# Eight gate/value pairs by seven products, weight bits joined in PSUM, and a down product that starts with two output blocks side by side

## The chip, the cores and the metric

One core of a Trainium2 chip runs the whole program. The metric is the device time of one execution in microseconds (us); the median of three runs counts. The engines are PE (TensorE: matmuls, whose results land in PSUM), DVE (VectorE), ACT (ScalarE), POOL (GpSimd) and SP, which issues the loads and stores. Each engine works through its own queue in order; an instruction that has to wait for another engine holds everything behind it in its queue.

## The reference

Attention with a bias from a small network (2 batches, 8 heads, 576 positions, head size 64), then two feed-forward blocks on the 1152 resulting rows of width 512:

```
x = attention(q, k, v, w1, b1, w2)                     # 1152 x 512
xn = x / rms(x) * rms_g
g, val = xn @ w_gate, xn @ w_val                       # 512 -> 1536, twice
y = (silu(g) * val) @ w_out                            # 1536 -> 512
r = max(y @ w_in, 0)                                   # 512 -> 2048
out = (s * r * r + b) @ w_out2                         # 2048 -> 512
```

The weights come as 64-bit floating-point numbers and are turned into 32-bit ones on the chip.

## The kernel before

The first 178 us are attention. After that PE works through the feed-forward blocks with weights as the stationary operand and 384 rows of the activations (a third of the 1152, called j = 0, 1, 2) as the moving one. To keep precision every operand is split in two, a rounded part (`hi`) and the remainder (`lo`), and each 128-deep step takes three matmuls: hi·hi, hi·lo and lo·hi (`mm3`, lines 588 to 593).

**The gated stage** makes 12 pairs m = 0 to 11 of one gate block and one value block (128 outputs each). Its smallest step is `prod` (line 613): six matmuls of 128x384, half the depth of 512. A pair done in the plain way takes 2 blocks x 3 thirds x 2 halves = 12 such steps (`whole`, line 693). `seven` (line 706) takes a fast matrix multiplication for the thirds j = 0 and 1: seven products in place of eight, of sums of weights (`t_sums`, `t_split`, lines 653 and 668) and of sums of activations (made once, `s_view`, in the buffer `reg`); with the four plain steps of j = 2 that is 11 steps: p1, p2, p5, p6, gate half, p7, gate half, value half, value half, p4, p3. Products p1, p6, p7 and p4 add up in one PSUM bank `a`, and between them ACT copies out what stands there (`snap`, line 646): p6 waits for the copy of p1, p7 for the copy of p6, p4 for the copy of p7. The copy of p6 has one step of PE in which to be made. `MIXED` (line 675) lists the pairs done so: 3, 5, 7, 9, 11.

Each block's weights are a *unit* of 512 KB, 2m the gate's and 2m + 1 the value's; units 24 on are those of the later products. A unit passes a load by SP (`w_fetch`), ACT's absolute value and POOL's clamp (`w_clamp`, lines 379 and 380), three DVE steps that join the bits (`bits_of`, lines 387, 388, 390, all in place in the tile `wa`), ACT's rounding to `whi` (line 402) and POOL's subtraction to `wlo` (line 405). `prep(q, p)` (line 677) sets which of these stands at step p of the pair ahead of pair q, with one table for a pair in `MIXED`, one for a pair behind one of these, one for the rest. `later(d, fn)` puts a piece of work into the queues d steps on; `up_gated` calls `due()` (the pieces whose time has come), then `prep`, then the PE step.

The product of gate and value is made on DVE (`times`, line 633). For m < `KEPT` = 7 it is split at once: DVE multiplies into the PSUM bank, ACT rounds from there, DVE subtracts. For the other five pairs DVE writes a plain tile, and `narrow` (line 796) splits it later, at steps 1 to 5 of the down product, 1152 columns at a time.

**The down product** (`down`, line 834) takes for each output block m = 0 to 3 the twelve results in three chunks i of four; a step (`slot`) is 12 matmuls of 384 columns. Before the change all chunks of a block are done before the next block. The second feed-forward block runs in two halves, each of eight `up_sq` blocks and a `down` of two chunks.

`bank()` (line 549) hands out the eight PSUM banks in turn: three of `psB`, four of `psC`, and `po`, the one bank of `psO` that attention used for its output.

Of the kernel before, what the change touches and what calls it, by code (L numbers as in the profile page):

```python
# [8 lines left out]
F32 = mybir.dt.float32  # L9
F32R = mybir.dt.float32r  # L10
I32 = mybir.dt.int32
U64 = mybir.dt.uint64
AF = mybir.ActivationFunctionType
ALU = mybir.AluOpType
# [3 lines left out]
P = 128  # L18
# [6 lines left out]
NT = B * S  # L25
DM = H * D
NKC = DM // P
# [24 lines left out]
def tile_kernel(ctx: ExitStack, tc: tile.TileContext, q, k, v, ltab, lg, cst, cst2, rms_g, wg, wv, wo, win, wo2, s_p, b_p, out):  # L52
    nc = tc.nc
# [24 lines left out]
    psO = pool(ctx, "psO", 1, space=PSUM)  # L78
# [41 lines left out]
    def batches(u):  # L120
        tt = TILES[u // 4]
        return [tt % 2] if tt < 8 else [0, 1]
# [106 lines left out]
    pos = {}  # L229
# [54 lines left out]
    def values_mm(u):  # L284
        hp = u % 4
        bs = batches(u)
        if hp == 0:
            pos[u // 4] = psO.tile([P, 512], F32, name="po")
        po = pos[u // 4]
        cols = P // len(bs)  # L290
        tl = pts.pop((u, 2))
        pm = [pts.pop((u, e)) for e in range(2)]
        for bi, b in enumerate(bs):
            c0 = bi * cols
            vt = vs[b * NP + hp]
            for c in range(NQC):
                for o in range(0, P, 32):
                    e, d = divmod(o, D)
                    dst = po[o:o + 32, hp * P + c0:hp * P + c0 + cols]
                    w, a = (vt[:, 4 * e + c, d:d + 32], pm[e][:, c * P + c0:c * P + c0 + cols]) if c < 4 else \  # L300
                        (vt[:, 8 + e, d:d + 32], tl[:, c0:c0 + cols])
                    nc.tensor.matmul(dst, w, a, start=c == 0, stop=c == NQC - 1, tile_position=(0, o))  # L302
# [51 lines left out]
    units = []  # L354
    for m in range(12):
        units += [wg[m], wv[m]]
    for m in range(NKC):
        units += [wo[m, 0, i] for i in range(3)]
    for half in range(2):
        units += [win[half * 8 + m] for m in range(8)]  # L360
        for m in range(NKC):
            units += [wo2[m, half, i] for i in range(2)]
    wst = {}
    wab = {}
    wpools = {}
# [17 lines left out]
    def bits_of(n):  # L383
        raw, w = wst[n]
        wst[n] = w
        a = w
        yield nc.vector.tensor_scalar(a, a, 3, 0x3FFFFFF8, op0=ALU.logical_shift_left, op1=ALU.bitwise_and)  # L387
        yield nc.vector.scalar_tensor_tensor(out=w, in0=raw[:, :, 1], scalar=-0x40000000, in1=a,  # L388
                                             op0=ALU.bitwise_and, op1=ALU.bitwise_or)
        yield nc.vector.scalar_tensor_tensor(out=w, in0=raw[:, :, 0], scalar=29, in1=w,  # L390
                                             op0=ALU.logical_shift_right, op1=ALU.bitwise_or)

    def w_bits(n):
# [3 lines left out]
    def w_split(n):  # L397
        if n < len(units):
            w = wst[n]
            hi = wpools["sp"].tile([P, 4 * P], F32R, name="whi")  # L400
            lo = wpools["sp"].tile([P, 4 * P], F32R, name="wlo")
            nc.scalar.copy(hi, w.bitcast(F32))  # L402
            step = 2 * P if n in FIRST_DOWN else 4 * P
            for c in range(0, 4 * P, step):
                nc.gpsimd.tensor_tensor(out=lo[:, c:c + step], in0=w[:, c:c + step].bitcast(F32),  # L405
                                        in1=hi[:, c:c + step].bitcast(F32), op=ALU.subtract)
            wst[n] = hi, lo
# [58 lines left out]
    for s in range(-2, NU + 1):  # L466
# [54 lines left out]
        if s == 26:  # L521
# [5 lines left out]
            reg = reg_p.tile([P, 6 * NT], F32R, name="reg", tag="reg")  # L527
# [13 lines left out]
    ff_p = pool(ctx, "ff", 1)  # L541
    t_p = ring(ctx, "t", 3)
    turn = [0]
    cur = [0]

    def ff(i, dtype=F32R):
        return ff_p.tile([P, NT], dtype, name="f", tag=f"f{i}")

    def bank():
        turn[0] += 1  # L550
        if turn[0] % 8 == 7:
            return psO.tile([P, 512], F32, name="po")
        if turn[0] % 2:
            return psB.tile([P, 512], F32, name="b")
        return psC.tile([P, 512], F32, name="c")

# [12 lines left out]
    def later(d, fn):  # L569
        late.append([d, fn])  # L570
# [9 lines left out]
    def slot(i):  # L580
        ahead(i)
        due()

    def take():
        w = wst.pop(cur[0])
        return w

    def mm3(ps, w, c, ah, al, first, last):
        hi, lo = w
        ws = slice(c * P, (c + 1) * P)  # L590
        nc.tensor.matmul(ps, hi[:, ws], ah, start=first, stop=False)  # L591
        nc.tensor.matmul(ps, hi[:, ws], al, start=False, stop=False)  # L592
        nc.tensor.matmul(ps, lo[:, ws], ah, start=False, stop=last)  # L593
# [7 lines left out]
            mm3(ps, w, c, src[0][:, c, cols(j)], src[1][:, c, cols(j)], c == 0, c == NKC - 1)  # L601
        return ps

    KEPT = 7
    ffs = {}
    sgs = {}

    def act_pair(m):
        if m not in ffs:
            ffs[m] = [ff(2 * m), ff(2 * m + 1)] if m < KEPT else [ff(2 * KEPT + m - KEPT, F32)]  # L610
        return ffs[m]
# [60 lines left out]
        nc.gpsimd.tensor_tensor(out=lo, in0=t, in1=hi.bitcast(F32), op=ALU.subtract)  # L672
        tsp[q, i] = hi, lo

    MIXED = (3, 5, 7, 9, 11)

    def prep(q, p):
        n = 2 * q
        if q in MIXED:
            do = {1: [(w_bits, n)], 2: [(w_clamp, n + 1)], 3: [(w_fetch, n + 2), (w_split, n)], 4: [(w_bits, n + 1)],  # L680
                  5: [(w_fetch, n + 3)], 6: [(t_sums, q, 0)], 7: [(t_sums, q, 1)], 8: [(t_split, q, 0)],
                  10: [(t_split, q, 1)], 11: [(w_split, n + 1)]}
        elif q - 1 in MIXED:
            do = {0: [(w_clamp, n)], 1: [(w_clamp, n + 1)], 2: [(w_bits, n)], 3: [(w_fetch, n + 2)],
                  4: [(w_bits, n + 1)], 5: [(w_fetch, n + 3)], 6: [(w_split, n)], 8: [(w_split, n + 1)],
                  9: [(w_clamp, n + 2)]}
        else:
            do = {1: [(w_bits, n)], 2: [(w_clamp, n + 1)], 3: [(w_fetch, n + 2), (w_split, n)], 5: [(w_bits, n + 1)],
                  6: [(w_fetch, n + 3)], 8: [(w_split, n + 1)], 9: [(w_clamp, n + 2)]}
        for fn, *arg in do.get(p, ()):  # L690
            fn(*arg)

    def whole(m, f, j):
        st = []
# [76 lines left out]
    def up_gated(n_m):  # L771
        last = NTT - 1
        subs = [(m, fn) for m in range(n_m)
                for fn in (seven(m) if m in MIXED else [h for f in range(2) for j in range(NJ) for h in whole(m, f, j)])]
        order = [0, 1, 2, 3, 6, 7, 8, 9, 12, 13, 4, 5, 10, 11]
        subs[:len(order)] = [subs[i] for i in order]
        start = [2 * 2 * NJ * m - len([x for x in MIXED if x < m]) for m in range(n_m + 1)]
        for t, (m, fn) in enumerate(subs):
            at = max(x for x in range(n_m) if start[x] <= t)
            due()  # L780
            prep(at + 1, t - start[at])
            if t in LATER:
                LATER[t][0](LATER[t][1])
            fn()
            if t == 0:
                finish_t(last)
                finish_b(last)
                finish_s(last)
                finish_n(last)
            if t == 6:  # L790
                finish_c(last)
        cur[0] = 2 * n_m
        place = {7: (reg, 0), 8: (reg, 1), 9: (reg, 2), 10: (14, 15), 11: (16, 17)}
        acts = [ffs[m] for m in range(KEPT)]

        def narrow(m, src):
            a, b = place[m]
            if m < 10:
                hh, hl = (reg[:, (2 * b + i) * NT:(2 * b + i + 1) * NT] for i in range(2))
            else:  # L800
                hh, hl = ff(a), ff(b)
            nc.scalar.copy(hh, src)
            nc.vector.tensor_tensor(out=hl, in0=src, in1=hh.bitcast(F32), op=ALU.subtract)
            acts[m] = hh, hl

        acts += [None] * (n_m - KEPT)
        for i, m in enumerate(range(KEPT, n_m)):
            later(i + 1, lambda m=m: narrow(m, ffs[m][0]))
        return acts

    sq_at = iter(list(range(16)) + [16, 17, 18] + list(range(13)))
# [21 lines left out]

    def down(acts, emit, tail=False):
        n = len(acts)
        for m in range(NKC):
            parts = [cols(j) for j in range(NJ)]
            if tail and m == NKC - 1:
                parts[1:] = [slice(TJ, NT - TAIL_N), slice(NT - TAIL_N, NT)]
            pss = [bank()[:, :cs.stop - cs.start] for cs in parts]  # L840
            for i in range(n // 4):
                w = take()
                for j, cs in enumerate(parts):
                    slot(j)
                    for c in range(4):
                        a = acts[4 * i + c]
                        mm3(pss[j], w, c, a[0][:, cs], a[1][:, cs],
                            i == 0 and c == 0, i == n // 4 - 1 and c == 3)
                    if i == n // 4 - 1:
                        emit(m, cs, pss[j])  # L850
                cur[0] += 1

    sg_p = ring(ctx, "sg", 4)
    ts_p = pool(ctx, "ts", 1)
# [1 line left out]
    acts = up_gated(12)  # L856
# [112 lines left out]
```

## Time and profile before

| what | value |
|---|---|
| three runs | 606.63, 607.23, 609.87 us; median 607.23 |
| the profiled execution | 606.63 us, of which the span of the trace is 604.9 us |
| PE busy in the span | 596.2 us (99%) |
| PEld, DVE, ACT, POOL busy | 534.3, 426.1, 324.5, 224.9 us |

PE's busy share counts matmuls that overlap one another, so it says little by itself. More telling is the distance from one matmul's start to the next one's, and the places where PE stood idle. All rows in the section on rows come from the one profiled execution.

### The profile page before, as it was taken

How to read it: one execution, taken by the hardware profiler on the slowest of the kernel's cores; microseconds unless marked ns; L12 is line 12 of the kernel's file. 1: busy time of each engine (PE TensorE's matmuls, PEld its weight loads, DVE VectorE, ACT ScalarE, POOL GpSimd, SP SyncE). 2: the span in 40 equal slices, each digit the busy share in tenths (PEclk: the TensorE clock that was granted, in tenths of full speed). 3: DMA queues.
4: the chain of work that ended last, by engine and by line, in shares of the span. 5: the costliest groups of instructions: out<-in, count | busy, mean ns of one | idle time of the engine just before them, and what ended most of it. 6: DMA issues, size and time to landing. Idle time of an engine off the chain costs nothing.

```text
span 604.9 us, 13376 instructions
## 1 busy us (share of the span) xinstructions
PE 596.2 (99%) x5400; PEld 534.3 (88%) x5400; DVE 426.1 (70%) x765; ACT 324.5 (54%) x670; POOL 224.9 (37%) x201
## 2 busy tenths in 40 slices
PE   8999999999999999999999999999999999999997
PEld 5466666667779999999999999999999999999997
DVE  7977888976877887676467745648887535888851
ACT  7887887887765355544346322245555235555210
POOL 0424334623437754344444233322224333222420
PEclk9999999999999999999999999999999999999999
DMA  7998544564112233223223133222223422222431
GB/s 215 267 320 234 158 149 142 159 209 136 37 40 69 70 104 105 71 74 130 76 70 105 71 105 104 70 71 70 69 71 106 139 70 70 69 70 71 144 101 52
DMA packets 25885, 67.52 MB, mean 112 GB/s; under 512 B 3136, under 2 KB 4704, under 8 KB 25824
## 3 DMA queue, kind: packets, MB, share of 16 engines
q1 hardware_dynamic: 25776, 66.66, 35.3%
q8 instruction: 42, 0.69, 0.5%
q14 instruction: 19, 0.16, 0.1%
q10 hardware_dynamic: 48, 0.02, 0.0%
HBM read 53.47 MB, written 10.83 MB: 106 GB/s over the span
## 4 chain that ended last, share of the span: by engine, by line
PE 70%; DVE 16%; ACT 7%; issue 5%; POOL 1%; DMA 1%; POOLq 0%; ACTq 0%; DVEq 0%
PE c L616 8%; PE po L302 7%; PE b L616 7%; PE a L244 6%; PE b L272 6%; PE c L593 5%; DVE f L827 5%; PE c L591 4%; PE c L592 4%; DVE hv L823 4%; PE b L591 3%; PE b L593 3%; PE b L592 3%; PE b L189 3%; ACT f L826 3%
## 5 line engine op out<-in xcount | busy, mean ns | idle before, releaser
L405 POOL TENSOR_TENSOR wlo<-wa,whi 128x512 fp32r<-128x512 f32 (+1 forms) x71 | 92.3, 1306 | 96.0 <-ACT whi L402 93.9
L380 POOL TENSOR_SCALAR wa<-wa 128x512 f32<-128x512 f32 x68 | 44.9, 660 | 145.6 <-ACT wa L379 143.0
L387 DVE TENSOR_SCALAR wa<-wa 128x512 int32<-128x512 int32 x68 | 44.2, 650 | 35.9 <-POOL wa L380 35.8
L256 DVE CUSTOM_DVE_ANT_0 sn<-a,bias 128x576 f32<-128x576 f32 x72 | 51.7, 753 | 20.9 <-PE a L244 11.8
L379 ACT ACTIVATE wa<-wraw 128x512 f32<-128x512 f32 x68 | 45.6, 671 | 28.7 <-DMA wraw<-in_wo 23.4
L616 PE MATMUL c<-xs,whi 128*128 128x384 f32 x228 | 57.9, 334 | 0.0
L263 ACT ACTIVATE pr<-sn,nm 128x576 f32<-128x576 f32 x72 | 56.2, 781 | 2.8 <-DVE nm L256 2.7
L176 POOL TENSOR_SCALAR hq<-tab,c_sb,thr 128x384 f32<-128x384 f32 (+17 forms) x24 | 45.3, 1895 | 28.7 <-PE b L189 28.7
L390 DVE SCALAR_TENSOR_TENSOR wa<-wraw,wa 128x512 int32<-128x512 int32 x68 | 54.3, 799 | 2.3
L388 DVE SCALAR_TENSOR_TENSOR wa<-wraw,wa 128x512 int32<-128x512 int32 x68 | 53.7, 789 | 2.3
L827 DVE SCALAR_TENSOR_TENSOR f<-hv,b_sb,f 128x384 fp32r<-128x384 f32 x48 | 39.6, 824 | 21.9 <-ACT f L826 21.9
L826 ACT ACTIVATE f<-hv,b_sb 128x384 fp32r<-128x384 f32 x48 | 29.7, 618 | 45.4 <-DVE hv L823 45.3
L402 ACT CAST whi<-wa 128x512 fp32r<-128x512 f32 x68 | 41.9, 616 | 21.3 <-DVE wa L390 20.0
L593 PE MATMUL c<-f,wlo 128*128 128x384 f32 (+1 forms) x150 | 50.8, 339 | 0.7 <-POOL wlo L405 0.7
L592 PE MATMUL c<-f,whi 128*128 128x384 f32 (+1 forms) x150 | 50.6, 337 | 0.0
L591 PE MATMUL c<-f,whi 128*128 128x384 f32 (+1 forms) x150 | 50.6, 337 | 0.0
L302 PE MATMUL po<-pt,vs 128*32 128x128 f32 (+1 forms) x1600 | 46.7, 264 | 0.0
L244 PE MATMUL a<-ks,q 64*64 64x352 f32 (+1 forms) x576 | 45.3, 416 | 0.5 <-ACT br L205 0.2
L281 ACT COPY pt<-b 128x512 f32<-128x512 f32 (+1 forms) x78 | 33.1, 434 | 20.3 <-PE b L272 20.1
L616 PE MATMUL b<-xs,whi 128*128 128x384 f32 x172 | 43.8, 335 | 0.0
L244 PEld LDWEIGHTS a<-ks,q 64*64 64x64 f32 x576 | 19.0, 132 | 28.0 <-issue 6.5
L302 PEld LDWEIGHTS po<-pt,vs 128*32 128x32 f32 x1600 | 37.6, 110 | 5.8 <-issue 5.7
(204 smaller groups left out, 1534.2 us busy)
## 6 DMA issues: line engine op xcount, KB each, us to landing
wraw<-in_wo SPq DMA_DIRECT2D x28, 512.0 KB, 3.5
bias<-rows SPq DMA_DIRECT2D x32, 288.0 KB, 4.3
rows<-br SPq DMA_DIRECT2D x28, 295.5 KB, 3.1
wraw<-in_win SPq DMA_DIRECT2D x16, 512.0 KB, 3.5
wraw<-in_wg SPq DMA_DIRECT2D x12, 512.0 KB, 3.5
wraw<-in_wv SPq DMA_DIRECT2D x12, 512.0 KB, 3.6
vs<-in_v SPq DMA_DIRECT2D x8, 320.0 KB, 7.2
ks<-in_k SPq DMA_DIRECT2D x8, 288.0 KB, 7.0
```

The costliest lines, as they stand in the source:

```text
L244: nc.tensor.matmul(ps[e][qc, f], qt[u // 4][ed, hp, qc], ks[b[i % len(b)] * NP + hp][ed, f], start=True, stop=True, tile_position=(e * D, ...
L256: nc.vector.tensor_tensor_reduce(out=sn, in0=ps, in1=bias[chunk(u)][:, h, :], scale=-1.0 / SCALE, scalar=3.0e38, op0=ALU.add, op1=ALU.min, ...
L263: nc.scalar.activation(prs[u][:, e * S:(e + 1) * S], sn, AF.Exp, bias=nm, scale=-1.0, accum_out=sums[u // 4][:, h:h + 1])
L302: nc.tensor.matmul(dst, w, a, start=c == 0, stop=c == NQC - 1, tile_position=(0, o))
L388: yield nc.vector.scalar_tensor_tensor(out=w, in0=raw[:, :, 1], scalar=-0x40000000, in1=a, op0=ALU.bitwise_and, op1=ALU.bitwise_or)
L390: yield nc.vector.scalar_tensor_tensor(out=w, in0=raw[:, :, 0], scalar=29, in1=w, op0=ALU.logical_shift_right, op1=ALU.bitwise_or)
L405: nc.gpsimd.tensor_tensor(out=lo[:, c:c + step], in0=w[:, c:c + step].bitcast(F32), in1=hi[:, c:c + step].bitcast(F32), op=ALU.subtract)
L591: nc.tensor.matmul(ps, hi[:, ws], ah, start=first, stop=False)
L592: nc.tensor.matmul(ps, hi[:, ws], al, start=False, stop=False)
L593: nc.tensor.matmul(ps, lo[:, ws], ah, start=False, stop=last)
L616: nc.tensor.matmul(ps, w[i][:, (c0 + c) * P:(c0 + c + 1) * P], a[h][c], start=first and c == 0 and i == 0 and h == 0, stop=c == 1 and i == ...
L827: nc.vector.scalar_tensor_tensor(out=hl[:, cols(j)], in0=g2, scalar=b_sb, in1=hh[:, cols(j)].bitcast(F32), op0=ALU.add, op1=ALU.subtract)
```

## The change

Eight pairs are done by seven products, 3 and 5 to 11. Pairs behind one another in the list get a table of their own, in which the value unit of a pair is split at that pair's own first step. For units 2 to 23 the three bit steps go through the PSUM bank `po`: the first two write there, the third reads it and writes `wa`. So the gated stage hands out seven banks, and `po` joins the turn when it is over. `KEPT` is 4: products are split at once for four pairs, and eight are split in the down product, at its steps 1 to 8. The down product takes the chunks of its first two output blocks by turns, (0,0), (1,0), (0,1), (1,1) and so on as (block, chunk), and then blocks 2 and 3 one after the other; the weights are loaded in that order. The split results lie in other buffers (`free`).

```diff
-            pos[u // 4] = psO.tile([P, 512], F32, name="po")
+            pos[u // 4] = psO.tile([P, 512], F32, name="po", tag="po")
...
-    for m in range(NKC):
-        units += [wo[m, 0, i] for i in range(3)]
+
+    def down_order(n):
+        return [(m, i) for i in range(n) for m in (0, 1)] + [(m, i) for m in (2, 3) for i in range(n)]
+
+    units += [wo[m, 0, i] for m, i in down_order(3)]
     for half in range(2):
         units += [win[half * 8 + m] for m in range(8)]
-        for m in range(NKC):
-            units += [wo2[m, half, i] for i in range(2)]
+        units += [wo2[m, half, i] for m, i in down_order(2)]
...
         a = w
-        yield nc.vector.tensor_scalar(a, a, 3, 0x3FFFFFF8, op0=ALU.logical_shift_left, op1=ALU.bitwise_and)
-        yield nc.vector.scalar_tensor_tensor(out=w, in0=raw[:, :, 1], scalar=-0x40000000, in1=a,
+        t = psO.tile([P, 4 * P], I32, name="pw", tag="po") if 1 < n < 24 else a
+        yield nc.vector.tensor_scalar(t, a, 3, 0x3FFFFFF8, op0=ALU.logical_shift_left, op1=ALU.bitwise_and)
+        yield nc.vector.scalar_tensor_tensor(out=t, in0=raw[:, :, 1], scalar=-0x40000000, in1=t,
                                              op0=ALU.bitwise_and, op1=ALU.bitwise_or)
-        yield nc.vector.scalar_tensor_tensor(out=w, in0=raw[:, :, 0], scalar=29, in1=w,
+        yield nc.vector.scalar_tensor_tensor(out=w, in0=raw[:, :, 0], scalar=29, in1=t,
                                              op0=ALU.logical_shift_right, op1=ALU.bitwise_or)
...
+    spare = []
...
-        if turn[0] % 8 == 7:
-            return psO.tile([P, 512], F32, name="po")
-        if turn[0] % 2:
+        if spare and turn[0] % 8 == 7:
+            return psO.tile([P, 512], F32, name="po", tag="po")
+        if turn[0] % (8 if spare else 7) in (1, 3, 5):
             return psB.tile([P, 512], F32, name="b")
...
-    KEPT = 7
+    KEPT = 4
...
-    MIXED = (3, 5, 7, 9, 11)
+    MIXED = (3, 5, 6, 7, 8, 9, 10, 11)
...
-        if q in MIXED:
+        if q in MIXED and q - 1 in MIXED:
+            do = {0: [(w_clamp, n)], 1: [(w_clamp, n + 1)], 2: [(w_bits, n)], 3: [(w_fetch, n + 2)],
+                  4: [(w_split, n), (w_bits, n + 1)], 5: [(w_fetch, n + 3)], 7: [(t_sums, q, 0), (t_sums, q, 1)],
+                  8: [(t_split, q, 0)], 10: [(t_split, q, 1)]}
+        elif q in MIXED:
...
+        if p == 0 and q - 1 in MIXED and q - 2 in MIXED:
+            w_split(n - 1)
...
+        turn[0] = turn[0] % 7
+        spare.append(0)
+        acts = [ffs[m] for m in range(KEPT)] + [None] * (n_m - KEPT)
+        free = [16, 17, 18] + list(range(2 * KEPT, KEPT + n_m))
...
         n = len(acts)
-        for m in range(NKC):
+        pss = {}
+        for m, i in down_order(n // 4):
...
-            pss = [bank()[:, :cs.stop - cs.start] for cs in parts]
-            for i in range(n // 4):
-                w = take()
...
+            if i == 0:
+                pss[m] = [bank()[:, :cs.stop - cs.start] for cs in parts]
+            w = take()
```

On DVE, the bit steps of unit 4, which stand between the multiplications and subtractions of pair 1. Before:

```order
L387 TENSOR_SCALAR wa<-wa 128x512
L388 SCALAR_TENSOR_TENSOR wa<-wraw,wa 128x512
L390 SCALAR_TENSOR_TENSOR wa<-wraw,wa 128x512
L638 TENSOR_TENSOR po<-po,sg 128x384
L642 TENSOR_TENSOR f<-po,f 128x384
```

and now:

```order
L390 TENSOR_SCALAR pw<-wa 128x512
L391 SCALAR_TENSOR_TENSOR pw<-wraw,pw 128x512
L393 SCALAR_TENSOR_TENSOR wa<-wraw,pw 128x512
L642 TENSOR_TENSOR c<-c,sg 128x384
L646 TENSOR_TENSOR f<-c,f 128x384
```

Nothing changes its place; the three steps no longer take both of their tensors from SBUF, where `wa` and `wraw` lie, and the product's bank is another one. The queue of DVE keeps this order up to pair 3.

On ACT, around the start of pair 7 (`wraw` and `wa` are the next pair's weights, `ut0` and `ut1` the copies of PSUM bank `a`, `th0` and `th1` the rounded sums of weights). Before, where pair 6 is a plain one:

```order
L671 CAST th0_4207<-ut2_4186 128x512
...
L402 CAST whi_4240<-wa_4100 128x512
L379 ACTIVATE wa_4251<-wraw_4152 128x512
L641 CAST f_4204<-c_4231 128x384
L648 COPY ut0_4263<-b_4254 128x384
L379 ACTIVATE wa_4251<-wraw_4176 128x512
L631 ACTIVATE sg_4274<-sg_4274 128x384
L648 COPY ut1_4295<-b_4254 128x384
L648 COPY ut0_4315<-b_4254 128x384
L402 CAST whi_4317<-wa_4251 128x512
```

and now, between pairs 6 and 7 that are both done by seven products:

```order
L675 CAST th0_4225<-ut2_4213 128x512
L766 ACTIVATE c_4135<-c_4135 128x384
L675 CAST th1_4244<-ut3_4214 128x512
L381 ACTIVATE wa_4256<-wraw_4168 128x512
L405 CAST whi_4259<-wa_4128 128x512
L652 COPY ut0_4271<-b_4263 128x384
L381 ACTIVATE wa_4256<-wraw_4193 128x512
L635 ACTIVATE sg_4282<-sg_4282 128x384
L652 COPY ut1_4304<-b_4263 128x384
L405 CAST whi_4306<-wa_4256 128x512
L652 COPY ut0_4329<-b_4263 128x384
```

The rounding of the product (`f_4204`) is gone from in front of the first copy; `th1` now stands behind the silu of the pair before; one `whi` has come between the second and the third copy.

On PE, the first matmul of each chunk of the down product for the blocks' first third (`f` and `reg` hold the split results, `whi` is the unit). Before, block 0 alone, then block 1:

```order
L591 MATMUL c_4843<-f_3427,whi_4791 128x384
...
L591 MATMUL c_4843<-f_3953,whi_4813 128x384
...
L591 MATMUL c_4843<-reg_2637,whi_4884 128x384
...
L591 MATMUL po_5011<-f_3427,whi_4942 128x384
```

and now:

```order
L595 MATMUL c_4889<-f_3429,whi_4837 128x384
...
L595 MATMUL b_4948<-f_3429,whi_4859 128x384
...
L595 MATMUL c_4889<-reg_2637,whi_4930 128x384
...
L595 MATMUL b_4948<-reg_2637,whi_4991 128x384
...
L595 MATMUL c_4889<-f_4975,whi_5050 128x384
```

The second chunk of results is wanted six steps after the start where it was three, the third twelve steps where it was six.

## Rows read from the trace of the kernel before

**Rows 1.** Busy time by stage: stretch, its length, PE, PEld, DVE, ACT, POOL, clock, DMA.

```profile
178.00:325.30 147.30, 146.17 (x846) 145.50 (x846) 103.11 (x165) 72.33 (x139) 74.17 (x67) 1.00 0.27 86
325.30:400.20 74.90, 74.90 (x434) 74.90 (x433) 43.55 (x55) 24.28 (x40) 24.00 (x24) 1.00 0.25 85
```

**Rows 2.** PE's waits from 178 us on: total, times, longest.

```profile
PE b L616 <- ACT ut L648: 1.0, 1, 1.0
PE c L593 <- POOL wlo L405: 0.7, 2, 0.4
```

**Rows 3.** Timeline of PE, pair 3 and the second block's first down product: start, duration.

```profile
212.68 0.33 PE L616 MATMUL c<-xs,wlo 128*128 128x384 f32 x1
...
219.96 0.34 PE L616 MATMUL b<-reg,tl 128*128 128x384 f32 x1
221.31 0.62 PE L616 MATMUL b<-reg,th 128*128 128x384 f32 x2 [1.01 <-ACT ut L648]
...
457.35 0.44 PE L593 MATMUL c<-f,wlo 128*128 128x384 f32 x1 [0.36 <-POOL wlo L405]
```

**Rows 4.** The chain that ended last, 218 to 226 us: start, length, what.

```profile
218.31 0.48 DVE b L638
...
219.19 0.63 ACT whi L402
219.82 0.56 ACT wa L379
...
220.40 0.48 ACT f L641
220.88 0.39 ACT ut L648
...
222.63 1.04 PE c L616 x6
```

**Rows 5.** DVE's instructions on `wa`: count, shortest/median/longest in ns.

```profile
L387 DVE TENSOR_SCALAR wa<-wa x68: 411/419/2051, 157.2 to 580.8; 128x512 int32<-128x512 int32 x68
L388 DVE SCALAR_TENSOR_TENSOR wa<-wraw,wa x68: 685/693/2223, 158.2 to 582.3; 128x512 int32<-128x512 int32 x68
L390 DVE SCALAR_TENSOR_TENSOR wa<-wraw,wa x68: 680/692/2211, 159.4 to 583.0; 128x512 int32<-128x512 int32 x68
```

**Rows 6.** Timeline of DVE, unit 4 and the product of pair 2.

```profile
194.29 2.05 DVE L387 TENSOR_SCALAR wa<-wa 128x512 int32<-128x512 int32 x1 [2.83 <-POOL wa L380]
...
199.54 0.55 DVE L638 TENSOR_TENSOR po<-po,sg 128x384 f32<-128x384 f32 x1
...
216.65 0.56 DVE L638 TENSOR_TENSOR c<-c,sg 128x384 f32<-128x384 f32 x1
```

**Rows 7.** Timeline of POOL beside unit 4.

```profile
196.01 2.04 POOL L438 TENSOR_TENSOR reg<-us,reg 128x768 fp32r<-128x768 f32 x1
```

**Rows 8.** DVE instructions with an operand in PSUM, by line; shortest/median/longest in ns.

```profile
L281 DVE COPY pt<-b x30: 679/685/692, 27.0 to 175.5; 128x512 f32<-128x512 f32 x30
L642 DVE TENSOR_TENSOR f<-c,f x11: 547/558/559, 190.9 to 267.5; 128x384 fp32r<-128x384 f32 x11
L638 DVE TENSOR_TENSOR c<-c,sg x10: 553/562/567, 189.7 to 266.4; 128x384 f32<-128x384 f32 x10
```

**Rows 9.** Timeline of ACT and of PE in pair 7: the copy of p6, and p7.

```profile
270.51 0.48 ACT L648 COPY ut<-b 128x384 f32<-128x384 f32 x1 [0.89 <-PE b L616]
...
271.35 0.51 PE L616 MATMUL b<-reg,th 128*128 128x384 f32 x2
```

**Rows 10.** The costliest groups of the page: busy, mean ns.

```profile
L405 POOL TENSOR_TENSOR wlo<-wa,whi 128x512 fp32r<-128x512 f32 (+1 forms) x71 | 92.3, 1306 | 96.0 <-ACT whi L402 93.9
```

**Rows 11.** The late splits in the down product, by line: shortest/median/longest in ns.

```profile
L803 DVE TENSOR_TENSOR reg<-f,reg x3: 1349/1789/1990, 327.6 to 331.3; 128x1152 fp32r<-128x1152 f32 x3
```

**Rows 12.** Timeline of the first down product: its last two late splits, its first matmul.

```profile
334.76 3.72 DVE L803 TENSOR_TENSOR f<-f 128x1152 fp32r<-128x1152 f32 x2
...
325.43 0.33 PE L591 MATMUL c<-f,whi 128*128 128x384 f32 x1
```

More of the change, by code (lines that the diff above doesn't have):

```diff
@@ L792, in up_gated, with narrow @@
         cur[0] = 2 * n_m
[L793 to L799, printed above, removed]
-            else:
-                hh, hl = ff(a), ff(b)
+        turn[0] = turn[0] % 7
+        spare.append(0)
+        acts = [ffs[m] for m in range(KEPT)] + [None] * (n_m - KEPT)
+        free = [16, 17, 18] + list(range(2 * KEPT, KEPT + n_m))
+        def narrow(m):
+            src = ffs[m][0]
+            if m < KEPT + 3:
+                hh, hl = (reg[:, i * NT:(i + 1) * NT] for i in (2 * (m - KEPT), 2 * (m - KEPT) + 1))
+            else:
+                at = 2 * (m - KEPT - 3)
+                hh, hl = ff(free[at]), ff(free[at + 1])
             nc.scalar.copy(hh, src)
@@ L804, in narrow @@
             acts[m] = hh, hl
-        acts += [None] * (n_m - KEPT)
         for i, m in enumerate(range(KEPT, n_m)):
-            later(i + 1, lambda m=m: narrow(m, ffs[m][0]))
+            later(i + 1, lambda m=m: narrow(m))
         return acts
@@ L839, in down @@
                 parts[1:] = [slice(TJ, NT - TAIL_N), slice(NT - TAIL_N, NT)]
-            pss = [bank()[:, :cs.stop - cs.start] for cs in parts]
-            for i in range(n // 4):
-                w = take()
[L843 to L851, printed above, removed]
+            if i == 0:
+                pss[m] = [bank()[:, :cs.stop - cs.start] for cs in parts]
+            w = take()
+            for j, cs in enumerate(parts):
+                slot(j)
+                for c in range(4):
+                    a = acts[4 * i + c]
+                    mm3(pss[m][j], w, c, a[0][:, cs], a[1][:, cs],
+                        i == 0 and c == 0, i == n // 4 - 1 and c == 3)
+                if i == n // 4 - 1:
+                    emit(m, cs, pss[m][j])
+            cur[0] += 1
     sg_p = ring(ctx, "sg", 4)
```

## The prediction

> **What bounds the kernel now.** I first read the table by stage: in the gated stage (178 to 325.3 us) PE is busy 146.2 of 147.3 us and in the first down product all of 74.9, with a granted clock of 1.00, the upper of the two levels (2.4 GHz), while DVE is at 103.1 and 43.6, ACT at 72.3 and 24.3, POOL at 74.2 and 24.0 [rows 1]. So PE is late everywhere; the others matter only where PE waits for them. The list of PE's waits gives three such places behind attention: one of 1.0 us for ACT's copy `ut` and two, 0.7 us in all, for a `wlo` of POOL [rows 2]. The timeline puts the first in pair 3, before p6, and the last two in the second matmul block's down products, of which one row stands for both [rows 3]. The chain of waits then gives the price of a step of six matmuls, 1.04 us [rows 4], or 0.1733 us for a matmul, start to start. That, and not the 0.33 us that a row shows for one matmul, is what a matmul left out is worth, because the rows overlap.
>
> **Fewer matmuls.** Five pairs by seven products become eight. Each of the three new ones takes 11 steps for 12: 3 x 6 = 18 matmuls, 3 x 1.04 = 3.12 us of PE. Nothing else in PE's work changes in amount: the down products have the same matmuls in another order. Since PE has no idle time there to hide it in, the whole 3.12 us comes off, unless new waits appear.
>
> **The bit steps in PSUM.** Now a unit's three steps take 0.42, 0.69 and 0.69 us at the median, but up to 2.05, 2.22 and 2.21 [rows 5]. Unit 4 shows the long ones: its steps begin at 194.29, and DVE gets to the next instruction only at 199.54, 5.25 us for 1.8 [rows 6]. POOL is then working on SBUF tiles: its 2.04 us instruction starts at 196.01 [rows 7], inside that stretch. DVE instructions that have a PSUM operand and at most one in SBUF show no such stretching in any of the groups that I list: 30 copies from PSUM between 679 and 692 ns, 11 subtractions between 547 and 559, 10 multiplications between 553 and 567 [rows 8], though POOL was busy for half of the gated stage [rows 1]. The new second and third steps are of that kind. The first, from SBUF into PSUM, does not occur in the trace: bounds are its median now, 0.42, and the PSUM copy of the same size, 0.69; a stretch to 2.05 can't be excluded either. I take 0.69, the row with a PSUM operand. So a unit costs 3 x 0.69 = 2.1 us where it cost 1.8 undisturbed and 5.25 at worst. The 0.3 us more, for 22 units, is DVE time beside PE's and costs nothing while DVE keeps up.
>
> The Trainium skill (SBUF — State Buffer, "Who interferes with whom") says that VectorE with two SBUF inputs, or in a mode that uses both of its ports, shares a port pair with GpSimd as an exclusive lock, and with at most one SBUF input outside these modes does not contend. By it the stretching goes from all three steps and the sum is the forecast's; without it the wait of pair 3 stays and the sum is the first rival's. The long rows of units like 4 agree with it; that a write to PSUM alone escapes, no run here shows yet.
>
> **Pair 3's wait.** From 219.96 to 221.31 PE takes 1.35 us for a step of 0.173: 1.18 us lost [rows 3]. The chain before it runs through DVE's product (218.31), ACT's `whi` and absolute value (219.19, 219.82), ACT's rounding of the last product of pair 2 (220.40), then the copy `ut` (220.88) [rows 4]. All this is DVE lag: bank `c`, whose last matmul starts at 212.68 [rows 3], is multiplied only at 216.65 [rows 6], about 3.6 us after it was there. DVE lagged because of the stretched bit steps (unit 4's alone put it back 5.25 - 2.1 = 3.2 us). Pair 2 is still split at once, and the order on DVE and ACT up to here is the same, so the copy still stands behind three roundings; but with the lag gone each follows its product. The copy has to be done 1.18 us earlier, and 3.2 us are given back. I count the whole 1.18 us.
>
> **Longer rows of pairs by seven products.** What is late next is the wait for the copies. The tightest is p7 behind the copy of p6: now the copy runs from 270.51 to 270.99 and p7 starts at 271.35, 0.36 us to spare [rows 9]. In the new order nothing stands between p6's end and this copy on ACT but an absolute value and a silu of the step before, queued 2 us earlier, and the rounding of the product is gone from ahead of it. The second is p6, which needs `th1` and `tl1`. These now stand behind the silu of p4, at the last step of the pair before. From p4's end there are 4 steps, 4.2 us, to p6; silu 0.5, cast 0.6, POOL's subtraction 1.3 as for `wlo` [rows 10], and about 0.2 for each hand-over make 3.0. So 1.2 us remain. The silu and cast figures are estimates from ACT's 0.48 us copy [rows 9] and 0.63 us `whi` [rows 4] of the same sizes. DVE in such a pair: two units 4.2, three sums 1.5 (an estimate, two 512-column additions at 0.69 rounded up), six products and sums of 0.56, 3.4 together [rows 8]: 9.1 of 11.4 us. POOL: four subtractions at 1.3 [rows 10] and two clamps that I take as no longer make at most 7.8. No engine exceeds the pair's 11 x 1.04 us, so I take nothing for it.
>
> **The down product.** Eight late splits in place of five. On DVE one takes 1.35 to 1.99 us, and the last two of now are done at 334.76 + 3.72 = 338.5, 13.1 us after the product's first matmul at 325.43 [rows 11, 12]; they are wanted at its seventh step (6 x 2.08 = 12.5) and, as third and fourth of four, up to 1.6 us into it. Five splits therefore just fit. Afterwards the first four are wanted at 12.5 us and the other four at 12 x 2.08 = 25 us. By today's pace four are done at about 11.3 us, and the other four, at 1.85 each with two further units of 1.8, some 11 us later, at 22. Both fit, so this edit costs nothing; without the turn-taking the eighth would be 10 us late. The weights stay ahead: a unit's bit steps are queued six steps, 12.5 us, before its use and need 1.8 + 0.63 + 1.3 = 3.7 us down to `wlo` [rows 4, 5, 10]. The second block's two waits of 0.7 us stay: the steps behind which they stand are the same. Seven banks for eight: a bank comes round 7 hand-outs later, a pair by seven products takes 5, so it is free for over 2 us before reuse. The bank `po` serves DVE alone while the stage lasts.
>
> **Sum.** 606.63 - 3.12 - 1.18 = 602.3 us on the profiled execution's own scale. That run is the lowest of the three, 0.6 under their median; between the two scales I say 602.6.
>
> **Rivals.**
> - *Pair 3's wait stays*, because the write into PSUM is stretched too or ACT's queue is what holds the copy: 606.63 - 3.12 = 603.5. For it: three roundings stand before the copy. Against it: the 3.6 us lag of DVE.
> - *Part is eaten by small new waits*: if p6 or p7 of the seven pairs after pair 3 lose 0.3 us each, about the 0.36 that p7 has to spare, 2.1 us: 602.3 + 2.1 = 604.4, or 605.6 with pair 3's wait as well. For it: the longer list of work on ACT. Against it: four such pairs behind a plain one run now without any wait.
> - *Slower*: work on the sums of weights falls behind, and every pair by seven products shows the wait that pair 3 shows now, since each starts from the lag of the one before. Seven more waits of 1.18 are 8.3 us: 606.63 - 3.12 + 8.3 = 611.8. The point from which it decides is 3.12 / 7 = 0.45 us a pair. For it: DVE at 9.1 of 11.4 us, and the cast `th1` behind a silu. Against it: 1.2 us to spare.
> - *More is gained*: the two waits for `wlo` go too, 602.3 - 0.7 = 601.6. Nothing in that stage changes but the phase.
>
> **Chances and range.** Forecast 0.53, pair 3's wait stays 0.14, small new waits 0.17, slower 0.09, more gained 0.07. The range 601.0 to 606.2 leaves out the slow case and a little below; the forecast's own range is 601.6 to 603.6. Half a per cent, about what a measurement of this kernel can tell from no change, is 3.0 us of 607.2: the forecast and the larger gain are faster, pair 3's wait staying (3.1 us) is at the border and is shared out, small waits are mostly the same. Faster 0.65, same 0.26, slower 0.09.
>
> **What would show it.** In the profile after: the gated stage some 4.3 us shorter than 147.3; no wait of PE for `ut` in pair 3; the bit steps into `pw` all near 0.7 us with no row at 2; PE's steps still 1.04 us; no idle time in the down product's seventh and thirteenth step. The forecast is wrong if PE waits for `ut`, `th` or `tl` in pairs 6 to 11, or if bit steps into PSUM reach 2 us.

## The result, and the profile after

The changed kernel takes 603.1 us in the median of six runs (601.69 to 604.34), the one before 607.55 (606.63 to 609.87); the ratio of the two is 0.9918, with a 95% interval of 0.9894 to 0.9943, or 3.5 to 6.4 us less. The forecast was 602.6 us, 601.0 to 606.2.

The profiled execution has a span of 601.3 us where the one before had 604.9. Its stages, from the first matmul of one to the first matmul of the next, in us:

| stage | before | after |
|---|---|---|
| attention, up to the first gated matmul | 178.26 | 179.11 |
| gated stage | 147.17 | 142.75 |
| first down product | 74.88 | 74.88 |
| second block, first up half | 49.92 | 49.92 |
| its down product | 50.59 | 50.57 |
| second up half | 49.92 | 49.92 |
| its down product, to PE's last end | 50.82 | 50.82 |
| from there to the end | 3.30 | 3.30 |

The three starts behind the first two rows, the gated stage's before and after and the first down product's after (the one before is in [rows 12]):

```profile
178.26 0.59 PE L616 MATMUL b<-xs,whi 128*128 128x384 f32 x2
...
179.11 0.59 PE L620 MATMUL b<-xs,whi 128*128 128x384 f32 x2
...
321.87 0.33 PE L595 MATMUL c<-f,whi 128*128 128x384 f32 x1
```

All of the gain, 4.42 us, is in the gated stage. Attention, whose instructions did not change, took 0.85 us longer in this execution, so the spans differ by 3.6 us only.

The table by stage, rounded to the same stretches as before (stretch, length, then busy time of PE, PEld, DVE, ACT, POOL, the clock, DMA), and the list of PE's waits from 178 us on:

```profile
179.10:321.90 142.80, 142.68 (x828) 142.33 (x827) 102.31 (x175) 76.91 (x145) 78.07 (x73) 1.00 0.28 89
321.90:396.70 74.80, 74.80 (x433) 74.80 (x432) 47.47 (x57) 27.52 (x43) 24.94 (x24) 1.00 0.26 85
```

```profile
PE b L597 <- POOL wlo L408: 0.7, 2, 0.4
```

Against [rows 1] PE is idle for 0.1 us in the gated stage where it was idle for 1.1, though ACT and POOL have some 4 us more to do there; against [rows 2] the wait for `ut` is gone and the two for `wlo` are left. The timeline of PE in pair 3 (start, duration):

```profile
219.77 0.33 PE L620 MATMUL c<-xs,wlo 128*128 128x384 f32 x1
219.94 0.51 PE L620 MATMUL c<-reg,th 128*128 128x384 f32 x2
...
220.81 0.33 PE L620 MATMUL c<-reg,tl 128*128 128x384 f32 x1
220.99 0.51 PE L620 MATMUL b<-reg,th 128*128 128x384 f32 x2
```

p6, the last row, starts 0.18 us after the matmul before it, where 1.35 us had passed [rows 3]. The copy it needs is made in time:

```profile
219.10 0.48 ACT L652 COPY ut<-b 128x384 f32<-128x384 f32 x1
```

It ends at 219.58, 1.4 us ahead of p6, although it still stands behind the roundings of pair 2's products. DVE's lag, from which the prediction derived the wait, is gone: the last matmul into pair 2's bank `c` and DVE's multiplication of that bank are

```profile
213.53 0.33 PE L620 MATMUL c<-xs,wlo 128*128 128x384 f32 x1
...
213.97 0.57 DVE L642 TENSOR_TENSOR c<-c,sg 128x384 f32<-128x384 f32 x1 [0.68 <-PE c L620]
```

0.44 us from start to start, where it was 216.65 - 212.68 = 3.97 before [rows 3, 6]; DVE now waits for PE there. And the bit steps that go through PSUM, with shortest, median and longest duration in ns:

```profile
L390 DVE TENSOR_SCALAR pw<-wa x22: 680/690/697, 184.5 to 304.0; 128x512 int32<-128x512 int32 x22
L391 DVE SCALAR_TENSOR_TENSOR pw<-wraw,pw x22: 695/695/697, 185.2 to 304.8; 128x512 int32<-128x512 int32 x22
L393 DVE SCALAR_TENSOR_TENSOR wa<-wraw,pw x22: 686/686/690, 185.9 to 305.5; 128x512 int32<-128x512 int32 x22
```

Where [rows 5] had rows of 2 us, all 66 are within 17 ns of each other.

### The profile page after: what moved, and what is told of

Same layout as the page of the kernel before. It is cut to its first block, busy times and chain, and to the rows that moved or that the text cites. A ratio compares the mean times of both kernels' runs of the same rounds, so it can differ in the third digit from the quotient of the medians.

```text
span 601.3 us, 13394 instructions
## 1 busy us (share of the span) xinstructions
PE 594.3 (99%) x5382; PEld 530.7 (88%) x5382; DVE 428.4 (71%) x777; ACT 332.5 (55%) x679; POOL 230.5 (38%) x207
## 4 chain that ended last, share of the span: by engine, by line
PE 73%; DVE 13%; ACT 5%; DMA 5%; issue 3%; POOL 1%; SPq 0%; ACTq 0%; POOLq 0%
PE c L620 13%; PE b L620 10%; PE po L302 6%; PE a L244 5%; DVE f L839 5%; PE c L597 5%; PE c L595 5%; PE c L596 5%; PE b L272 4%; DVE hv L835 4%; PE b L597 4%; PE b L595 4%; PE b L596 4%; ACT f L838 3%; DMA vs<-in_v 2%
## 5 line engine op out<-in xcount | busy, mean ns | idle before, releaser
L620 PE MATMUL c<-xs,whi 128*128 128x384 f32 x212 | 53.9, 334 | 0.0
L390 DVE TENSOR_SCALAR wa<-wa 128x512 int32<-128x512 int32 x46 | 30.2, 657 | 27.5 <-POOL wa L382 27.5
L281 ACT COPY pt<-b 128x512 f32<-128x512 f32 (+1 forms) x78 | 33.1, 434 | 20.3 <-PE b L272 20.1
L272 PEld LDWEIGHTS b<-ident,pr 128*128 128x128 f32 x288 | 30.8, 140 | 12.2 <-issue 9.6
L176 DVE TENSOR_SCALAR hq<-tab,c_sb,thr 128x448 f32<-128x448 f32 (+17 forms) x87 | 39.9, 516 | 0.0
```

The source lines that it names most:

```text
L176: eng.tensor_scalar(hq, src, w1_sb, thr[:, n:n + 1], op0=ALU.mult, op1=ALU.max)
L272: nc.tensor.transpose(pT[:, c * P:(c + 1) * P], pr[:, o:o + P], ident)
L620: nc.tensor.matmul(ps, w[i][:, (c0 + c) * P:(c0 + c + 1) * P], a[h][c], start=first and c == 0 and i == 0 and h == 0, stop=c == 1 and i == ...
```

## The experiments

Ten kernels, each run beside the kernel before; the ratios are to that. Attention differs by up to 2.3 us between profiles of the same instructions (below), so the stages tell more than the times.

### Bit steps in place again

```diff
-        t = psO.tile([P, 4 * P], I32, name="pw", tag="po") if 1 < n < 24 else a
+        t = a
```

> The changed kernel with the three bit steps of every unit in place in SBUF again, nothing else. Theory (pair 3 waited because stretched bit steps put DVE behind): the long rows (up to 2.2 us) come back, DVE is late before pair 3, PE waits there for the copy `ut` about 1.2 to 1.3 us, so the gated stage goes from 142.75 to about 144.0 us and the kernel loses 1.3 us; the later pairs may wait too, since DVE then needs up to 5.2 us for a unit. Rival (the wait went by another part: the seven banks, or the fewer splits): gated stage stays at 142.8 us and no wait in pair 3.

Measured: 604.46 us, ratio 0.9936 [0.9922, 0.9951]; gated stage 144.05 us, 1.30 more than the changed kernel's. DVE's long rows are back, and so is PE's wait, in pair 3 only:

```profile
L390 DVE TENSOR_SCALAR wa<-wa x68: 410/420/2052, 156.2 to 576.0; 128x512 int32<-128x512 int32 x68
```

```profile
PE b L620 <- ACT ut L652: 1.0, 1, 1.0
PE b L597 <- POOL wlo L408: 0.7, 2, 0.4
```

DVE's lag is back with them: the last matmul into pair 2's bank `c` starts at 211.97, and DVE multiplies 3.96 us later:

```profile
215.93 0.56 DVE L642 TENSOR_TENSOR c<-c,sg 128x384 f32<-128x384 f32 x1
```

So the stretched bit steps made that wait. All 45 steps in this trace that took over 15% longer than the shortest of their line overlap an instruction of POOL. In the changed kernel 40 of the 66 steps through PSUM overlap one by more than 0.1 us, and none of them is stretched. The later pairs don't need the PSUM detour: they ran without a wait here too.

### The PSUM detour alone

The kernel before with the lines for `pw` and for seven banks, and none of the others.

> The kernel before with the bit steps of units 2 to 23 through the PSUM bank and so seven banks in the gated stage, nothing else: five pairs by seven products. Theory: the wait in pair 3 goes and nothing else, gated stage 147.17 - 1.3 = 145.9 us, the kernel faster by 1.3 us (ratio 0.998). Rival: the wait of 1.2 to 1.3 us stays, because three roundings stand before the copy in ACT's queue: 147.2 us.

Measured: 605.81 us, ratio 0.9973 [0.9959, 0.9988]; gated stage 145.88 us. Of PE's waits from the gated stage on only the two for `wlo` remain:

```profile
PE b L595 <- POOL wlo L406: 0.7, 2, 0.4
```

Hence the detour is worth 1.29 us without the other edits, and the rest of the gated stage's gain, 145.88 - 142.75 = 3.13 us, is that of the 18 matmuls together with the edits that go with them.

### Seven products split at once

```diff
-    KEPT = 4
+    KEPT = 7
...
-        free = [16, 17, 18] + list(range(2 * KEPT, KEPT + n_m))
+        free = [14, 15, 16, 17]
```

> The changed kernel with seven products split at once again and five late (pairs 4, 5 and 6 get their three roundings on ACT and three subtractions on DVE back in the gated stage). Theory (the margins of p6, 1.2 us, and of p7, 0.35 us, hold three roundings of 0.48 us that wait for DVE only in part): waits in pairs 5 to 7 of 0 to 0.5 us each, in all under 1.5 us; down product unchanged at 74.9 us. Rival (late splitting is what made the row of pairs possible): about 1.2 us in each of pairs 5, 6 and 7, 3.6 us in all.

Measured: 604.26 us, ratio 0.9936 [0.9921, 0.995]; gated stage 143.65 us, 0.90 more; first down product 74.88. Two waits show, 0.21 us in pair 6 and 0.45 in pair 7; the second, in PE's and DVE's timelines:

```profile
267.29 0.34 PE L620 MATMUL c<-xs,wlo 128*128 128x384 f32 x1
267.91 0.61 PE L620 MATMUL c<-reg,th 128*128 128x384 f32 x2 [0.28 <-DVE f L646]
```

```profile
267.29 0.56 DVE L646 TENSOR_TENSOR f<-c,f 128x384 fp32r<-128x384 f32 x1 [0.28 <-ACT f L645]
```

It is not the copies that are late but the bank: p5 begins a bank in which the split of the pair before is still read by DVE's subtraction. Pair 5 has no such wait: the pair ahead of it, 4, is split at once too, but is a plain one. Late splitting multiplies out of the bank once and frees it.

### The copy of p6 three times

```diff
             def go():
-                st["u2"] = snap(1, st["a"])
+                for _ in range(3):
+                    st["u2"] = snap(1, st["a"])
```

> The changed kernel with the copy of p6 made three times in each of the eight pairs. Theory (p7 has 0.35 us to spare behind this copy): two more copies, which follow each other on ACT at 0.38 us, take 0.76 us, so p7 waits about 0.4 us in each pair, 8 x 0.4 = 3.3 us in all, gated stage 146.0 us. Rival (p7 does not follow closely on the copy): 142.8 us, no wait.

Measured: 610.49 us, ratio 1.0054 [1.0032, 1.0076]; gated stage 149.46 us, 6.71 more. Pair 5, ACT and PE:

```profile
247.73 1.50 ACT L652 COPY ut<-c 128x384 f32<-128x384 f32 x3 [0.89 <-PE c L620]
```

```profile
248.40 0.34 PE L620 MATMUL b<-xs,wlo 128*128 128x384 f32 x1
249.29 0.62 PE L620 MATMUL c<-reg,th 128*128 128x384 f32 x2 [0.55 <-ACT ut L652]
```

Every one of the eight pairs waits, 0.886 - 0.173 = 0.71 us between starts, not 0.4: three copies into one tile take 1.50 us, 0.51 apart, and not 0.38. So the two more take 1.02, of which 0.35 was spare, which leaves 0.67. Eight waits of 0.71 make 5.7; the stage lost another 1.0, 0.12 at each restart. The mechanism is that of the theory, the price was put too low.

### Block by block, with eight late splits

```diff
-        return [(m, i) for i in range(n) for m in (0, 1)] + [(m, i) for m in (2, 3) for i in range(n)]
+        return [(m, i) for m in range(4) for i in range(n)]
...
-            later(i + 1, lambda m=m: narrow(m))
+            later(i // 2 + 1, lambda m=m: narrow(m))
```

> The changed kernel with the down products done block by block again, (0,0), (0,1), (0,2), (1,0) and so on, and the eight late splits queued two a step at steps 1 to 4, as the chunks are wanted at steps 3 and 6. Theory (eight late splits need the turns of two blocks): the first four are done some 10 us after the product's first matmul and wanted at 6.2 us, the last some 20 us after it and wanted at 14 us; PE waits 5 to 8 us in all, down product from 74.9 to 80 to 83 us, the change's gain is gone or nearly. Rival (the splits are hidden either way): 74.9 us.

Measured: 605.16 us, ratio 0.9959 [0.9944, 0.9974]; first down product 76.97 us, 2.09 more. PE waits for the splits at the step that wants the second chunk and again at the third's:

```profile
328.76 0.34 PE L595 MATMUL c<-f,whi 128*128 128x384 f32 x1
329.57 0.44 PE L596 MATMUL c<-f,whi 128*128 128x384 f32 x1 [0.47 <-DVE f L816]
```

```profile
328.17 3.88 DVE L816 TENSOR_TENSOR f<-f 128x1152 fp32r<-128x1152 f32 x3
...
333.76 3.03 DVE L816 TENSOR_TENSOR f<-f 128x1152 fp32r<-128x1152 f32 x2
```

The turns are needed, but for 2.1 us and not for 5 to 8. Queued two a step, the splits take less time than I had counted: the last ends at 336.79, 16.1 us after the product's start at 320.66, where I had put it at 20 us; most of the eight took 1.35 us, for which I had 1.85.

### The turns alone

The kernel before with the down product's new order and nothing else.

> The kernel before with the down products' first two output blocks by turns (and their weights loaded in that order), nothing else. Theory (the turns only give the late splits more time, and five were in time already): first down product 74.9 us, the gated stage 147.2, no difference clear of the runs' spread. Rival (the turns are worth something by themselves, for the bank or the weights): one of the down stages shorter than 74.88, 50.59 or 50.82 us by more than 0.1.

Measured: 607.04 us, ratio 1.0001 [0.9986, 1.0016]; gated stage 147.18, down products 74.88, 50.57 and 50.79. The turns are worth nothing while only five products are split late.

### Nine pairs

```diff
-    MIXED = (3, 5, 6, 7, 8, 9, 10, 11)
+    MIXED = (3, 4, 5, 6, 7, 8, 9, 10, 11)
```

> The changed kernel with pair 4 by seven products too, so nine in a row from 3 to 11. Theory (a step of six matmuls is worth 1.04 us while the copies keep up): gated stage 142.75 - 1.04 = 141.7 us, waits under 0.3 us. Rival (pair 3 is still split at once, and its roundings stand before pair 4's copies, as in the kernel with seven split at once): waits of 0.5 to 1.3 us in pair 4, so nothing is gained.

Measured: 601.75 us, ratio 0.9909 [0.9879, 0.9938]; gated stage 142.04 us, 0.71 less than the changed kernel's. Of the 1.04 us, 0.33 is lost where pair 4's p5 begins a bank (and at the restart behind it):

```profile
230.51 0.34 PE L620 MATMUL c<-xs,wlo 128*128 128x384 f32 x1
230.89 0.61 PE L620 MATMUL b<-reg,th 128*128 128x384 f32 x2
```

```profile
230.27 0.56 DVE L646 TENSOR_TENSOR f<-b,f 128x384 fp32r<-128x384 f32 x1 [0.27 <-ACT f L645]
```

That is the bank of the test with seven splits, read by DVE until 230.83: pair 3 is done by seven products and split at once, as pairs 5 and 6 were there.

### Ten pairs

```diff
+    MIXED = tuple(range(2, 12))
```

> The changed kernel with pairs 2 and 4 by seven products too, ten in a row from 2 to 11. Theory: two steps fewer, 142.75 - 2.08 = 140.7 us, less a wait of 0.5 to 1.5 us in pair 2, whose sums of activations POOL finishes only some 2 us before it would start and whose products, like those of pairs 0 to 3, are split at once: 141 to 142 us. Rival (POOL's sums come later still): PE waits 3 us or more in pair 2, 143.5 us or more, slower than the changed kernel.

Measured: 605.6 us, ratio 0.9968 [0.9952, 0.9984]; gated stage 145.72 us, 3.0 more than the changed kernel's. The rival came about in its time and cause, with a wait of 2.4 us where it had 3 or more: POOL's last sums of activations end at 203.4, DVE and ACT queue behind them, and p6 of pair 2 waits for its copy:

```profile
203.43 1.50 DVE L667 TENSOR_TENSOR ut<-wa,ut 128x256 f32<-128x256 f32 x1 [1.74 <-POOL reg L441]
```

```profile
207.37 0.34 PE L620 MATMUL b<-reg,tl 128*128 128x384 f32 x1
209.96 0.79 PE L620 MATMUL c<-reg,th 128*128 128x384 f32 x2 [2.26 <-ACT ut L652]
210.54 0.53 PE L620 MATMUL c<-reg,tl 128*128 128x384 f32 x1
```

The wait is 2.59 - 0.17 = 2.42 us. But 145.72 is 4.7 us above 141.0, which is the 142.04 of nine pairs less one more step; the rest follows in the last section.

### The second unit in halves

```diff
-FIRST_DOWN = (24, 44, 60)
+FIRST_DOWN = (24, 44, 45, 60, 61)
```

> The changed kernel with POOL's subtraction for the second unit of each down product of the second block done in two halves, as it is for the first. Theory (each of these down products loses 0.53 us because the whole subtraction, 1.3 us, is awaited where its first half would do): the two waits shrink to nothing, the stages of 50.57 and 50.82 us to 50.1 and 50.3, 1.0 us in all. Rival (POOL or ACT is late by more than half a subtraction): the waits stay.

Measured: 600.94 us, ratio 0.9894 [0.9867, 0.9921]; the two down products of the second block 50.04 and 50.29 us. PE no longer waits for `wlo`. POOL's row, as two halves, beside the whole one of the changed kernel:

```profile
451.35 1.51 POOL L408 TENSOR_TENSOR wlo<-wa,whi 128x256 fp32r<-128x256 f32 x2 [2.56 <-ACT whi L405]
```

```profile
452.35 1.36 POOL L408 TENSOR_TENSOR wlo<-wa,whi 128x512 fp32r<-128x512 f32 x1 [2.56 <-ACT whi L405]
```

The two halves take longer together, yet the first is there 0.6 us sooner, which is what PE wanted: 0.53 us gained in each.

### Nine pairs and the halves

Both edits together.

> The changed kernel with nine pairs by seven products (3 to 11) and the second unit of each down product of the second block split in halves. Theory (the two touch different stages): gated stage 142.04 and down stages 50.04 and 50.29 us as each showed alone, 1.77 us off the changed kernel's 601.3 us span beside what attention varies, a median about 601 us, faster than the changed kernel and than the one before. Rival: one of the two gives back what it gained, gated stage 142.75 or down stages 50.6 and 50.8.

Measured: 600.57 us (six runs, 599.5 to 602.4), ratio 0.9895 [0.9874, 0.9916]; gated stage 142.07, down products 50.00 and 50.27. Each keeps what it gained, 0.68 + 0.57 + 0.55 = 1.80 us against the changed kernel's stages. It is the fastest of the kernels by its stages; in times it can't be told from the one with the halves alone.

## Why the prediction was right

The result lies in the range and on the forecast's mechanism.

- *18 matmuls, 3.12 us.* 3.13 us by the two kernels that both have the detour and differ in the other edits. The step of six stayed at 1.04 us.
- *Pair 3's wait, 1.18 us.* It went whole, and returned with the bit steps in place. The stage gained 1.30 by it: I had counted the idle time between two starts, and the first matmuls behind a wait are slow too, by 0.12 us, as the eight waits of the copy test show again. With this 3.13 + 1.29 is the 4.42 us measured, where the sum had 4.30.
- *Stretching of DVE.* The price of a step through PSUM was taken as 0.69 us, and it is 0.69. What no row showed, a write from SBUF alone into PSUM, escapes the stretching too: 680 to 697 ns in 22 cases, 11 of them beside an instruction of POOL for more than 0.1 us. The rule of the Trainium skill (SBUF — State Buffer, "Who interferes with whom"), that VectorE with at most one SBUF input outside its two-port modes does not contend with GpSimd, is borne out by these rows; and DVE's late splits, which have two SBUF inputs, still vary:

```profile
L816 DVE TENSOR_TENSOR f<-f x5: 1347/1352/2449, 331.2 to 339.7; 128x1152 fp32r<-128x1152 f32 x5
```

- *Rows of pairs by seven products cost nothing.* PE shows no wait in any of the eight. The margin of p7 is as read before [rows 9]; here pair 6, ACT's copy and PE's p7:

```profile
257.58 0.48 ACT L652 COPY ut<-c 128x384 f32<-128x384 f32 x1 [0.89 <-PE c L620]
```

```profile
258.43 0.51 PE L620 MATMUL c<-reg,th 128*128 128x384 f32 x2
```

0.37 us to spare. That this margin is real and guarded by nothing else the copy test showed. The second margin, p6 behind the sum `tl1`, is 1.6 us in pair 6 (`tl1` is done at 254.76, p6 starts at 256.35) where I had 1.2. A third guard I had passed over: with seven banks, splitting seven products at once costs 0.9 us by a bank that comes free too late, although I had put a bank's reuse at over 2 us of slack. That slack fails where a pair by seven products follows another one that is split at once: pairs 6 and 7 with seven split, pair 4 with nine pairs, pairs 3 and 4 with ten. In the changed kernel no pair stands so. Here I was lucky: the prediction counted on late splitting, `KEPT` = 4, for ACT's queue and not for the bank.

- *The down product costs nothing.* 74.88 us both times. The eight late splits are done at 338.28 + 3.72 = 342.0, 20.1 us after the start at 321.87 (22 expected) and before the 25 at which the last four are wanted:

```profile
338.28 3.72 DVE L816 TENSOR_TENSOR f<-f 128x1152 fp32r<-128x1152 f32 x2
```

The remark that without the turns the eighth would be 10 us late was too dark as a price: with the splits queued two a step PE lost 2.1 us. Without the turns and with one a step, as the remark had it, nothing was run.
- *The two waits for `wlo` stay.* They did, 0.53 us each, and were to be had by halving one subtraction; I had left them as given.

The profile's span shrank by 3.6 us only, because attention took 0.85 us longer in it. That was no part of the sum; the same instructions vary as much from one execution to another, as the next section but one shows.

## What to carry to other kernels

Where PE is the bound, price an edit by the distance between matmul starts and look for PE's few waits; each here had one instruction of another engine behind it, and the one in pair 3 a lag that arose 20 us earlier, in an instruction stretched by a neighbour. A scratch tile in PSUM took the VectorE steps here out of GpSimd's way; its price was 0.27 us more for the first step of each unit, which DVE had to spare, and one bank. Work moved to a later stage needs its deadline moved too: the three further late splits gained 0.90 us with the turns, the turns alone gained nothing, and the splits without them lost 2.09 us in the down product, more than they gain.

## What the runs showed of the hardware

A wait of PE costs more than its length. After waits of 0.7 us the restart cost 0.12 us more. After the 2.4 us of the kernel with ten pairs the granted clock fell from 1.00 to 0.54 in the next stretch of 3 us, near the lower of its two levels (1.2 GHz); matmuls started 0.32 us apart until 213.4, and 0.17 apart again from 213.7 on, 3.8 us after PE had gone on. The table by stretches (length, PE, PEld, DVE, ACT, POOL, clock, DMA):

```profile
207.00:210.00 3.00, 0.74 (x6) 0.42 (x4) 1.91 (x4) 2.52 (x6) 2.70 (x3) 1.00 0.00 0
210.00:213.00 3.00, 3.00 (x10) 3.00 (x11) 2.83 (x6) 1.82 (x4) 1.01 (x2) 0.54 0.01 3
213.00:216.00 3.00, 3.00 (x17) 3.00 (x17) 2.28 (x4) 0.77 (x2) 1.29 (x1) 0.89 0.68 186
216.00:219.00 3.00, 3.00 (x19) 3.00 (x19) 2.11 (x5) 1.36 (x3) 1.29 (x1) 1.00 0.48 164
```

Ten matmuls in 3 us instead of some 17: that, with two waits of 0.2 and 0.45 us for p5's bank in pairs 3 and 4, is the rest of the 4.7 us.

Attention, with the same instructions in all twelve profiles, took 177.55 to 179.87 us up to the first gated matmul, while stages without a change repeated to 0.05 us. So in the profiles the spread arises there. It does so at attention's two ends: from its 893rd matmul to its 2826th, of 2974, all twelve profiles take 109.51 us, while the 893rd starts 65.2 to 67.0 us after the beginning and the last stretch takes 2.6 to 3.5 us. What varies there, and whether it makes up the spread of the times of a kernel's runs, some 3 us, is not shown.
